# A spectral filter and a gated projection on one core: input weights requested one filter copy later, one product ahead of a transpose, second batch's units on other steps

## The chip, the cores and the metric

One core of one Trainium2 chip. The metric is device microseconds of a whole execution. The kernel before takes 787.34 us (median of 3 runs, 786.94 to 787.37).

The names used below: PE is the tensor engine (PEld its loading of weights), DVE the vector engine, ACT the scalar engine, POOL the general-purpose engine that also issues the casting DMAs, SP the engine of the sync queue. A DMA lands when the profile records its completion. The granted clock is the share of the full tensor-engine clock that the profile records as granted; 0.50 is the half clock. A turn (`a0_turn`, `z_turn`) is a transpose on PE.

## The reference

Eight sequences of 3008 tokens of 256 channels are filtered in the frequency domain, then go through a two-layer projection with a swish gate.

```python
X = np.fft.rfft(x, axis=1)                       # x: 8 x 3008 x 256
y = np.fft.irfft(X * (filt_r + 1j * filt_i), n=3008, axis=1)
h = y.reshape(24064, 256) @ w_in                 # w_in: 256 x 2048
g = h / (1 + np.exp(-beta * h))
out = g @ w_out                                  # w_out: 2048 x 256
```

## The kernel before

The transform is split by factors 47 and 64. The first batch's transform runs alone (the prologue, 0 to 37 us). Then a main part of 752 steps starts: in step s, 128 columns of `w_in` for a block of 512 tokens (`hps`), the gate on the scalar engine (`gT`), and two steps later the product with `w_out` (`acc`). Everything of the next batch's transform is placed on chosen steps of that stream. A batch is one of the eight sequences. `b` in the code counts from 0, so `b == 1` is the second batch.

The filters arrive by 24 DMAs on the sync queue, four for each of six units. Pool copies each unit's half to the other partitions (`spread`), and issues the casting DMAs (input weights `win_sb`, inputs `xg`) in the same order of program:

```python
    for u in range(3):
        spread(u)
    nc.gpsimd.dma_start(win_sb[:], moe_w_in.rearrange("(dc p) f -> p dc f", p=P))
    spread(3)
    spread(4)
    load_x(1, 0)
    spread(5)
    for g in range(1, 4):
        load_x(1, g)
    load_wout(0)          # on the sync queue, behind the filters
    load_wout(WG)
    scale_wout(0)         # on Pool: wout_sb = ws / beta
    scale_wout(WG)
    # ...
    a0_turn(4)
    a0_turn(5)
    s2_0(3)               # product with t2, then two vector products with the filters (pq_t)
    unit(2)
    # ... to s2_0(5), unit(4); then the last unit and the way to the first hps:
    s5 = [lps.tile([P, KU, P], F32, name="lp", tag="lp") for _ in range(NDC)]
    s3_0(NUN - 1, s5)     # lp: needs both vector products of unit 5
    # ... z_turn (zp), f4 (fp), then step 0 of the main part
```

The second batch's frequency units each take 2.07 us of the vector engine, and they sit on fixed steps:

```python
            s23_steps(1, [o + r for r in (21, 23, 26, 28, 30, 32, 35, 37, 39, 41, 44, 46)], 5, 1)
            # ...
            s4_steps(1, [o + 67 + (i * 12) // 15 for i in range(16)], 2)
```

## Time and profile before

| What | Before |
|---|---|
| span of the profiled run | 785.2 us |
| TensorE (PE) busy | 770.6 us |
| first hps / first acc | 36.84 / 40.76 us |
| input weights: issued / landed | 21.13 / 31.22 us |
| last filter copy on Pool starts | 30.99 us |

The head of the profile's page of the kernel before: busy time per engine, its share of the span, and instructions.

```profile
span 785.2 us, 15235 instructions
...
PE 770.6 (98%) x6046; PEld 545.0 (69%) x6046; DVE 446.7 (57%) x713; ACT 553.1 (70%) x814; POOL 150.5 (19%) x154
```

PE bounds the kernel, so what counts is where PE waits. The waits of PE, before (total us, times, longest):

```profile
PE lp L444 <- DVE pq_t L435: 3.0, 1, 3.0
...
PE acc L781 <- DVE ost L112: 0.9, 1, 0.9
...
PE ps L570 <- DVE b_t L588: 0.4, 1, 0.4
...
PE hps L763 <- ACT y L110: 0.2, 1, 0.2
```

The largest is in the prologue, and the other three shown are all that PE waits after the prologue. Busy time and gaps are not exact here, because the modelled end of a matmul can lie after the start of the next: the bar of two matmuls at 79.07 us is 0.38 us long, and the next matmul starts 0.22 us after their first. That will matter below.

The chain of waits, before, from 20 to 34 us (start, length, what), shows what the 3.0 us wait hangs on:

```profile
22.26 8.61 DMA fi_sb<-in_filt_i_dram
...
30.99 1.05 POOL fi_sb L473
...
32.06 1.30 DVE pq_t L435
...
33.40 0.41 PE lp L444 x4
```

The last filter DMA takes 8.61 us, where the DMAs of fi_sb whose landing the profile can match have a median of 4.2 us. The DMA packets tell why. They are counted here from the DMA records by start time; queue 1 is the sync queue (filters, output weights: 1 KB and 4 KB packets), queue 0 is Pool's (here 4 KB packets of the input weights).

```
before     queue 1: 1 KB / 4 KB packets   queue 0: 4 KB packets
23 to 24 us        71 / 29                        10
24 to 25 us        10 /  8                        37
25 to 26 us         0 /  0                        53
26 to 27 us        33 /  0                        44
27 to 28 us        41 /  0                        44
28 to 29 us        43 /  0                        44
```

The input weights take the DMA engines just as the last filter DMA is due. The wait has a second cost. The timeline by stretches, before (length, busy time of each engine, granted clock, DMA share, GB/s):

```profile
31.13:34.54 3.41, 0.99 (x15) 0.83 (x16) 1.77 (x3) 0.66 (x2) 2.35 (x4) 1.00 1.09 299
34.54:37.95 3.41, 3.37 (x32) 2.63 (x30) 2.63 (x9) 1.96 (x4) 2.56 (x2) 0.50 1.07 213
```

In the first stretch PE works 0.99 us of 3.41; in the next the granted clock is 0.50. The stretch at half clock is 3.41 us long. In both traces, before and after, the granted clock changes only at whole multiples of 3.413 us after its first record: before, the first record is at 7.24 us and the changes are 8 and 9 multiples later (34.54 and 37.95 us); after, it is at 5.26 us and they are 9 and 10 later (35.98 and 39.40 us). A stretch from one multiple to the next is called a window below.

### The profile page before, as it was taken

The page shows a single profiled execution, that of the slowest core. Times are in us where ns is not written, and L with a number is a line of the kernel's source. Part 1 is how long each engine was busy: PE and PEld are TensorE (multiplying, and loading weights), DVE is VectorE, ACT ScalarE, POOL GpSimd, SP SyncE. Part 2 cuts the span into 40 slices and gives each one's busy share as a digit, 9 for nine tenths or more (in the row PEclk, how much of TensorE's full clock was granted, in tenths as well). Part 3 has the DMA queues.
Part 4 walks back from the last instruction along what each step waited for, and adds up shares of the span by engine and source line. Part 5 has one row for each costly group of instructions (what it writes and reads, how often), then busy time and mean ns, then how long its engine had stood idle before and what let it go on. Part 6 is the DMA issues. An engine that isn't in the chain of part 4 may idle for free.

```text
span 785.2 us, 15235 instructions
## 1 busy us (share of the span) xinstructions
PE 770.6 (98%) x6046; PEld 545.0 (69%) x6046; DVE 446.7 (57%) x713; ACT 553.1 (70%) x814; POOL 150.5 (19%) x154
## 2 busy tenths in 40 slices
PE   8799999999999999999999999999999999999997
PEld 5566667766677666866678666786667766676665
DVE  8769754777557665566655665466655666321001
ACT  6676767767676766777667776677766777777776
POOL 6713400332012220122201222012200222000000
PEclk9999999999999999999999999999999999999999
DMA  9965586233931349123580416612164111500101
GB/s 182 241 187 122 116 229 169 68 88 99 247 85 51 96 125 252 42 76 108 114 243 28 120 61 159 197 56 86 48 189 119 63 48 48 156 28 28 55 28 55
DMA packets 84139, 88.51 MB, mean 113 GB/s; under 512 B 5772, under 2 KB 74380, under 8 KB 84068
## 3 DMA queue, kind: packets, MB, share of 16 engines
q1 hardware_dynamic: 79892, 73.81, 31.4%
q0 software_dynamic: 4032, 13.60, 10.4%
q8 instruction: 47, 0.77, 0.4%
q14 instruction: 24, 0.20, 0.1%
q10 hardware_dynamic: 144, 0.13, 0.0%
HBM read 54.47 MB, written 46.66 MB: 129 GB/s over the span
## 4 chain that ended last, share of the span: by engine, by line
PE 93%; DVE 2%; DMA 2%; SPq 0%; ACT 0%; issue 0%; POOL 0%; DVEq 0%; POOLq 0%; ACTq 0%
PE acc L781 41%; PE hps L763 41%; PE ps L554 3%; PE ps L622 2%; DMA fi_sb<-in_filt_i_dram 2%; PE ps L600 2%; PE ps L570 2%; DVE b_t L585 0%; DVE a_t L584 0%; SPq L91 0%; DVE b_t L588 0%; PE tp L400 0%; PE ps L405 0%; DVE u L224 0%; PE zp L400 0%
## 5 line engine op out<-in xcount | busy, mean ns | idle before, releaser
L772 ACT ACTIVATE gT<-hps,beta_sb 128x512 bf16<-128x512 f32 x752 | 516.9, 687 | 214.2 <-PE hps L763 211.1
L781 PE MATMUL acc<-wout_sb,gT 128*128 128x256 bf16 x3008 | 453.2, 272 | 0.9 <-DVE ost L112 0.9
L763 PE MATMUL hps<-y,win_sb 128*128 128x512 bf16 (+7 forms) x1728 | 448.6, 352 | 0.2 <-ACT y L110 0.2
L781 PEld LDWEIGHTS <-gT 128*128 128x128 bf16 x3008 | 286.8, 98 | 124.4 <-issue 2.3
L589 POOL TENSOR_TENSOR yh<-a_t,b_t 128x512 bf16<-128x512 f32 x84 | 106.3, 1266 | 426.1 <-DVE b_t L588 426.1
L763 PEld LDWEIGHTS <-win_sb 128*128 128x128 bf16 x1728 | 164.8, 98 | 24.8 <-DVE y L114 0.3
L112 DVE COPY ost<-acc 128x512 f32<-128x512 f32 (+1 forms) x94 | 60.0, 680 | 137.8 <-PE acc L781 137.8
L112 DVE CAST a<-ps 96x512 bf16<-96x512 f32 x107 | 72.8, 685 | 52.0 <-PE ps L554 47.9
L114 DVE TENSOR_SCALAR y<-ps 128x376 bf16<-128x376 f32 (+2 forms) x128 | 63.2, 511 | 62.0 <-PE ps L622 59.0
L584 DVE TENSOR_TENSOR a_t<-ps,fr_sb 128x512 f32<-128x512 f32 x84 | 58.1, 692 | 69.2 <-PE ps L570 68.6
L585 DVE SCALAR_TENSOR_TENSOR b_t<-ps,fi_sb 64x512 f32<-64x512 f32 x84 | 58.2, 693 | 1.1
L588 DVE TENSOR_TENSOR b_t<-ps,fi_sb 64x512 f32<-64x512 f32 x84 | 57.4, 684 | 1.1
L112 DVE CAST z<-ps 128x512 bf16<-128x512 f32 x72 | 49.3, 684 | 1.7 <-PE ps L600 0.8
L622 PEld LDWEIGHTS <-zz 96*128 96x128 bf16 x448 | 29.7, 97 | 22.9
L554 PE MATMUL ps<-xg,t 94*96 94x512 bf16 x112 | 42.1, 381 | 0.1
L622 PE MATMUL ps<-t,zz 96*128 96x94 bf16 x448 | 34.7, 205 | 0.0
L570 PE MATMUL ps<-a,t 128*128 128x256 bf16 x168 | 32.1, 273 | 0.4 <-DVE b_t L588 0.4
L600 PE MATMUL ps<-yh,t 128*128 128x256 bf16 x168 | 32.1, 273 | 0.0
L600 PEld LDWEIGHTS <-t 128*128 128x128 bf16 x168 | 16.2, 98 | 17.7
L570 PEld LDWEIGHTS <-t 128*128 128x128 bf16 x168 | 16.0, 98 | 15.3 <-DVE b_t L588 0.6
L171 POOL DMA_DIRECT2D xg<-in_x_dram x24 | 12.4, 519 | 56.5 <-PE ps L554 56.5
L554 PEld LDWEIGHTS <-t 94*96 94x96 bf16 x112 | 13.7, 123 | 10.2
(94 smaller groups left out, 179.0 us busy)
## 6 DMA issues: line engine op xcount, KB each, us to landing
out_dram<-ost SPq DMA_DIRECT2D x42, 512.0 KB, 3.0
d<-a SPq DMA_DIRECT2D x28, 384.0 KB, 4.5
a<-d SPq DMA_DIRECT2D x28, 384.0 KB, 5.4
d<-z SPq DMA_DIRECT2D x28, 384.0 KB, 3.9
zz<-d SPq DMA_DIRECT2D x28, 384.0 KB, 6.7
xg<-in_x_dram POOLq DMA_DIRECT2D x24, 384.0 KB, 6.4
out_dram<-ost SPq DMA_DIRECT2D x9, 256.0 KB, 3.5
ws<-in_moe_w_out_dram SPq DMA_DIRECT2D x4, 512.0 KB, 9.1
```

The source lines that it names most:

```text
L112: nc.vector.tensor_copy(dst, src)
L114: nc.vector.tensor_scalar_mul(dst, src, scale)
L554: nc.tensor.matmul(ps[:KP], lhsT=t1[:], rhs=xg[b, g][:NP, jj : jj + 2, :], start=True, stop=True)
L570: nc.tensor.matmul(ps[:, e, :], lhsT=t2[:, k0 + e, :], rhs=st["a2", b, g][:, kk + e, :], start=True, stop=True,)
L584: nc.vector.tensor_tensor(a_t[:], ps[:], fr_sb[:, ks, :], ALU.mult)
L585: nc.vector.scalar_tensor_tensor(b_t[:M], ps[M:], -1.0, fi_sb[M:, ks, :], ALU.mult, ALU.mult)
L589: nc.gpsimd.tensor_tensor(yh[:], a_t[:], b_t[:], ALU.add)
L600: nc.tensor.matmul(ps[:, e, :], lhsT=t3[:, 2 * i + e, :P], rhs=yh[:, e, :], start=True, stop=True)
L622: nc.tensor.matmul(ps[:, e, :NP], lhsT=zz[:, j0 % JG + e, dc * P : (dc + 1) * P], rhs=t4[:], start=True, stop=True,)
L763: nc.tensor.matmul(hps[:, pos - t0 : pos - t0 + ln], lhsT=win_sb[:, dc, fb * P : (fb + 1) * P], rhs=ys[b][:, dc, n0 : n0 + ln], start=(dc ...
L772: nc.scalar.activation(gT[:], hps[:], ACT.Silu, scale=beta_sb[:, fb : fb + 1])
L781: nc.tensor.matmul(acc_of(i, tb)[:, tb % 2, :], lhsT=blk[i * NFB + fb][:, tb * P : (tb + 1) * P], rhs=wout_sb[:, fb, :], start=(fb == 0 an ...
```

## The change

The intent is to let the filters finish before the input weights start, to give the vector engine unit 3's product sooner, and to take the second batch's vector work away from the steps where PE needs the vector engine for something else.

```diff
-    for u in range(3):
+    for u in range(4):
         spread(u)
     nc.gpsimd.dma_start(win_sb[:], moe_w_in.rearrange("(dc p) f -> p dc f", p=P))
-    spread(3)
     spread(4)
-    load_x(1, 0)
     spread(5)
-    for g in range(1, 4):
+    for g in range(4):
         load_x(1, g)
@@
     a0_turn(4)
-    a0_turn(5)
     s2_0(3)
     unit(2)
+    a0_turn(5)
@@
-            s23_steps(1, [o + r for r in (21, 23, 26, 28, 30, 32, 35, 37, 39, 41, 44, 46)], 5, 1)
+            s23_steps(1, [o + r for r in (22, 24, 26, 28, 30, 34, 36, 38, 40, 42, 44, 46)], 5, 1)
@@
-            s4_steps(1, [o + 67 + (i * 12) // 15 for i in range(16)], 2)
+            s4_steps(1, [o + 66 + (i * 12) // 15 for i in range(16)], 2)
```

## The prediction

> **What bounds the kernel.** PE: 770.6 of 785.2 us busy (engine table). The waits of PE in order of time: after 37 us only 0.42 us at 66.2, 0.93 at 79.1 and 0.19 at 128.5, so the rest is a fixed stream of matmuls. The prologue is a latency chain. Its largest PE wait is 2.95 us before the last filter product's turn (lp, 33.40 us), back through the vector product (pq_t, waits 2.29) and Pool's copy of fi_sb (waits 3.08) to the last filter DMA: issued 22.3, landed 30.9; the one before landed at 25.8. By DMA packets, the input weights (win, 1 MB, issued 21.13) move from 23.8 to 29.5 us: with both queues full, about 44 packets of 4 KB (win) and 43 of 1 KB (filter) start per us, one for one, so the filter gets a fifth of the bytes. [...] The wait also halves the granted clock from 34.5 to 38.0 us[...].
>
> **What the change does.** No work is added or removed.
> 1. win is issued about 23.35 instead of 21.13 us, so its packets start about 26.0, when the filters (140 KB left at 24 us, 215 KB/us) are through. Last filter landing: 30.9 to about 26.3. Pool's last copy ends 28.5 instead of 32.0.
> 2. s2_0(3) ahead of a turn: vector work starts 0.44 us earlier. Last product ends about 30.6 instead of 33.3; lp 2.75 us earlier, no half clock (about 1 us more). First hps could start near 33.3 instead of 36.84.
> 3. Batch 1's units on steps 22 to 46 leave the vector engine (2.07 us per unit) free at 33 for the accumulator copies, and its last stage ends a step before block 5 reads it: the 0.42, 0.93 and 0.19 us should go, 1.5 us together.
>
> **What is given back.** From 25 to 41 us the DMA engines are full in both versions (215 KB/us; win, x of batch 1, output weights), while PE now wants the data 3 to 4 us earlier. Estimates from the packet rates: win lands about 33.4; x group 0 about 35.4 (needed 34.8), so s1 gains only 2.9 us. Worst is the second output-weight block: before, the x requests came at 32 us and left its queue free at 32 to 34 us; now they come from 28.5, behind win without a gap, so the 1 KB packets get 42 KB/us and it lands about 42 instead of 37.2. Its scaling on Pool takes 1.9 us, so acc of fb=4, at 45.5 before and wanted near 42.5, waits until 44: a new PE wait of about 1.5 us. Net prologue gain 1.4 us.
>
> **Prediction.** 787.3 - 1.4 - 1.5 = 784.4 us; 8 in 10: 782.6 to 786.1. Faster by over 2%: 0.5%; within 2%: 99%; slower: 0.5%.
>
> **Right if** the waits for fi_sb and lp vanish, no half clock near 35 us, first hps near 33.5; a PE wait on xg or at acc behind Pool's wout scaling near 42 to 44 us; none near 66, 79, 128 us. **Wrong if** the output weights land in time (gain 4 to 5 us), or if the filters still lag behind win, the clock still halves, or later output-weight blocks stall too (little gain).

## The result and the profile after

The changed kernel takes 783.96 us (median of 4 runs, 782.81 to 785.03), before 787.31 us. The ratio is 0.9958, 95% interval 0.994 to 0.9976. Ratios here are the mean time of one kernel's runs over that of the other's of the same rounds, so not quite the ratio of the medians quoted. A second set on another chip gave 783.30 against 786.93 us, ratio 0.9956. The result is clear of noise, and inside the 2% band that counts as the same.

The four runs fall apart in two pairs: 782.81 and 783.08 us with a mean granted clock of 0.999 in both, 785.03 and 784.84 us with 0.998 and 0.996. The profiled run is one of the slower pair, so the profile shows less than the median gain.

The same lines after (source lines above are two lower after the change). The head of the page:

```profile
span 783.2 us, 15238 instructions
...
PE 769.8 (98%) x6046; PEld 543.7 (69%) x6046; DVE 446.9 (57%) x713; ACT 552.3 (71%) x814; POOL 150.6 (19%) x154
```

The waits of PE, after:

```profile
PE hps L761 <- DMA win_sb<-in_moe_w_in_dram: 1.8, 1, 1.8
...
PE lp L444 <- DVE pq_t L435: 0.2, 1, 0.2
PE ps L552 <- DMA xg<-in_x_dram: 0.2, 1, 0.2
```

The wait at lp is down from 2.95 to 0.20 us, and the three waits of the main part are gone (the list has no line for them). A new one stands at the first hps: PE now waits for the input weights. The PE timeline, after, around it (start, length, what, and idle time before it in brackets):

```profile
31.05 0.62 PE L444 MATMUL lp<-t,pq_t 128*128 128x128 bf16 x8 [0.20 <-DVE pq_t L435]
31.82 1.07 PE L400 MATMUL zp<-ident,y 128*128 128x128 bf16 x16
32.85 1.10 PE L405 MATMUL fp<-t,zz 96*128 96x94 bf16 x16
35.74 0.84 PE L761 MATMUL hps<-y,win_sb 128*128 128x512 bf16 x2 [1.79 <-DMA win_sb<-in_moe_w_in_dram]
```

lp is 2.35 us earlier than before (33.40), but the first hps only 1.10 us. In this run the window with little PE work has merely moved (stretches, after):

```profile
32.57:35.98 3.41, 1.62 (x24) 1.05 (x22) 2.16 (x8) 1.70 (x4) 1.96 (x2) 1.00 1.06 212
35.98:39.40 3.42, 3.26 (x18) 1.94 (x17) 1.37 (x2) 0.95 (x2) 0.00 (x0) 0.50 1.06 212
```

The half clock now falls on the first steps of the main part, where PE has more to do than before. The first acc starts at 40.86 us against 40.76: in the profiled run the whole prologue part is worth nothing. The gain of that run appears later. Starts of gate activations (gT, counted from 0, one for each step) in the main part, from the traces, in us:

```
                     first hps  first acc   gT 21    gT 81   last gT
before                 36.84      40.76     63.45   129.70   778.58
after                  35.74      40.86     63.56   127.73   776.61
after - before         -1.10      +0.10     +0.11    -1.97    -1.97
```

From gT 21 to gT 81 the change gains 2.08 us; after that nothing moves. So the second batch's steps are worth 2.08 us, and the prologue 0 to 2 us, depending on the run.

Why did the input weights come so late? The issue is where I expected it (23.48 us), but the transfer took longer: the DMA issues after 21 us, with KB and median us to landing, before and then after:

```profile
win_sb<-in_moe_w_in_dram POOLq DMA_DIRECT2D x1, 1024.0 KB, 10.1
ws<-in_moe_w_out_dram SPq DMA_DIRECT2D x2, 512.0 KB, 12.8
```

```profile
ws<-in_moe_w_out_dram SPq DMA_DIRECT2D x2, 512.0 KB, 7.7
win_sb<-in_moe_w_in_dram POOLq DMA_DIRECT2D x1, 1024.0 KB, 12.2
```

The output weights (`ws`) got faster and the input weights slower. By packets, after:

```
after      queue 1: 1 KB / 4 KB packets   queue 0: 4 KB packets
25 to 26 us       188 /  1                         0
26 to 27 us       254 /  0                         0
27 to 28 us       344 /  0                         0
28 to 29 us       187 /  0                        29
29 to 30 us         3 /  0                        49
30 to 31 us         5 /  0                        49
```

The first packet of the input weights starts at 28.37 us, 4.9 us after its issue; the output weights, requested at 22.92 and 23.54 us on the other queue (the second 0.06 us after the input weights), run nearly whole ahead of it, at up to 344 KB/us.

### The profile page after: what moved, and what is told of

It is laid out like the page before. It is cut to its first block, busy times and chain, and to the rows that moved or that the text cites. A ratio compares the mean times of both kernels' runs of the same rounds, so it can differ in the third digit from the quotient of the medians.

```text
span 783.2 us, 15238 instructions
## 1 busy us (share of the span) xinstructions
PE 769.8 (98%) x6046; PEld 543.7 (69%) x6046; DVE 446.9 (57%) x713; ACT 552.3 (71%) x814; POOL 150.6 (19%) x154
## 4 chain that ended last, share of the span: by engine, by line
PE 95%; DMA 2%; POOL 1%; DVE 1%; issue 1%; SPq 0%; ACT 0%; DVEq 0%; POOLq 0%
PE acc L779 42%; PE hps L761 42%; PE ps L552 3%; PE ps L620 2%; PE ps L598 2%; PE ps L568 2%; DMA xg<-in_x_dram 1%; DMA fr_sb<-in_filt_r_dram 1%; POOL fi_sb L473 1%; POOL fr_sb L472 1%; PE tp L400 0%; SPq L91 0%; PE ps L405 0%; DVE u L224 0%; DVE u L145 0%
## 5 line engine op out<-in xcount | busy, mean ns | idle before, releaser
L620 PEld LDWEIGHTS <-zz 96*128 96x128 bf16 x448 | 29.7, 97 | 22.9
```

What stands on the lines that cost most here:

```text
L620: nc.tensor.matmul(ps[:, e, :NP], lhsT=zz[:, j0 % JG + e, dc * P : (dc + 1) * P], rhs=t4[:], start=True, stop=True,)
```

## The experiments

Theory A. The two output-weight requests, in line behind the filters, hold the DMA engines until 28.3 us; the input weights follow, and PE waits for them. The wait leaves one window with little PE work (1.62 us of 3.41 in the profiled run), and the clock is halved in some runs. That it depends on where the windows happen to lie is my supposition; the traces show only that they lie differently, from 7.24 us on before and from 5.26 us on after. The steps give a fixed 2.1 us.

Rivals. B: the input weights start late because their request, made by a busy Pool, takes that long. C: the spread of the runs has nothing to do with the clock. D: the gain in the main part depends on the prologue.

### e1: the new steps alone

```diff
-            s23_steps(1, [... 21, 23, 26, 28, 30, 32, 35, 37, 39, 41, 44, 46 ...], 5, 1)
+            s23_steps(1, [... 22, 24, 26, 28, 30, 34, 36, 38, 40, 42, 44, 46 ...], 5, 1)
-            s4_steps(1, [o + 67 + ...], 2)
+            s4_steps(1, [o + 66 + ...], 2)
```

> The kernel before with only the second batch's units on their new steps; the first batch's order untouched. If the step part alone gives what the trace of the full change shows after the first accumulation (from 0.11 us behind to 1.97 us ahead), the span falls by about 2.1 us, as one narrow group of runs with a mean granted clock of 0.998 as before. If the gain depends on the new order of the first batch, less than 1 us.

Measured: 784.97 us against 787.09 (ratio 0.997, 0.9953 to 0.9986), 2.1 us by medians. In its trace gT 21 to gT 81 takes 64.16 us, before 66.25, after 64.17: 2.09 us, the same as in the full change. D falls. The runs were not narrow (783.8 to 786.69), nor were those of before on that chip (785.89 to 789.4). The profiled run, at 782.0 us of span, happened to have no half clock in the prologue: its first acc starts at 39.63 us instead of 40.76. Of those 1.1 us lp accounts for 0.2; I put the rest down to the clock. The kernel before has this chance too: on that chip its two fastest runs (785.89 and 786.11) have a granted clock of 0.999, its two slowest (789.35 and 789.4) 0.996 and 0.994.

### e2: the prologue's changes alone

The first two parts of the diff above, and not the steps.

> The kernel before with only the two changes of the first batch (input weights behind the fourth copy, fourth unit ahead of a turn). Theory[...]: the runs fall in two groups, one within 0.3 us of before with granted clock 0.998 or lower, one about 2 us faster with 0.999. Rival (the spread of the changed kernel comes from the steps or from DMA): one narrow group.

Measured: 785.44 us against 787.09 (0.9975, 0.9958 to 0.9993): 1.65 us by medians. The two groups did not appear: the runs spread from 784.41 to 786.91 us with clocks of 0.998 to 1.0. The profiled run had no half clock and still waited 1.7 us for the input weights and 1.1 us for x. So the clock is one source of spread and the landing of DMAs is another; here my expectation was too simple. The steps (2.1) and the prologue (1.65) add up to 3.8 us, where the full change measured 3.4 (medians); the intervals are wider than the difference.

### e3 and e7: idle matmuls in the new wait

```diff
         late.append((0, h, e, ps))
+    spin_late = zps.tile([P, 512], F32, name="zp", tag="zp")
+    for _ in range(6):
+        nc.tensor.matmul(spin_late[:], lhsT=rest[:, :P], rhs=rest[:], start=True, stop=True)
```

> The changed kernel with six idle matmuls (0.22 us each at full clock) between the first batch's last transform and the wait for the input weights. Theory: [...] filled, the half clock is gone in every run, all runs fall in the fast group, about 781 us of span (782.8 to 783.1 of time). Rival (the half clock comes from an earlier wait, or the two groups have another cause): still two groups, or no change.

> The changed kernel with six idle matmuls once more, so that it stands on the same chip as its neighbours: about 4.5 us faster than before, runs within 0.8 us of each other.

Measured: e3 782.85 us, runs from 782.43 to 783.18, ratio 0.9943 (0.9928 to 0.9957). e7, on another chip, 783.57 us, from 783.07 to 783.65, ratio 0.9956 (0.9943 to 0.9968). Filling the wait took the runs near 785 us away and narrowed the range from 2.2 us (changed kernel) to 0.8 and 0.6 us. e6 below has the same idle matmuls, and its five runs spread over 1.4 us (782.49 to 783.88). Taken together, three of the nine runs of the changed kernel (with e9) lie above 784.8 us, and none of the 16 of e3, e6 and e7. This supports the clock against C; the traces say more on it in the last section. A smaller gain on e7's chip than e3's is left unexplained, except that in its profiled run x landed 0.7 us later.

### e4: output weights requested after the input weights

```diff
+    held = consts.tile([1, 2], F32, name="held", tag="held")
+    nc.sync.dma_start(held[:], fi_sb[M : M + 1, 4 * KU, 0:2])   # waits for Pool's copy of unit 4
     load_wout(0)
     load_wout(WG)
```

> The changed kernel with the two output-weight requests held until Pool has copied unit 4's filters (about 26.5 us), so that they are asked for after the input weights. Theory A (the 1 MB of output weights already in the other queue keeps the engines until 28.3 us): the input weights start to move near 26 us and land near 33.5 instead of 35.7, the first matmul of the main part starts near 34, and the second output-weight block, then sharing with x, lands near 42 us, with a wait of 1 to 2 us at the accumulation of block 4. Rival B (the request itself takes 4.6 us to its first packet because Pool is busy): they still start near 28 and land near 35.7 us.

Measured: 782.87 us (0.9943, 0.9925 to 0.9961). The input weights' first packet starts at 24.87 us, 1.6 us after the issue (in the changed kernel 4.9), though Pool copies as before: B falls. They land at 32.02 us and the first hps starts at 33.84. One wait of PE in its list is much longer than in the changed kernel (there 0.2 us):

```profile
PE ps L554 <- DMA xg<-in_x_dram: 1.1, 1, 1.1
```

The wait for the input weights is gone, the wait for x is 1.1 us, and the second output-weight block lands at 41.77 us, near the prediction's 42. The wait of 1.5 us that was predicted for it at the fifth acc is only 0.21 us: that acc starts at 43.79 us (predicted 44), but PE, which has waited 1.1 us for x, comes for it at 43.58 us and not at 42.5. This kernel has the order of transfers that my prediction described, and it is no better than the one that does not: 782.87 against 782.85 us for e3 on the same chip.

### e5: idle matmuls in the old wait, old order

```diff
-    s3_0(NUN - 1, s5)
+    s3_0(NUN - 1, s5, 12)      # 12 matmuls of 512 columns between its two halves; with the new steps
```

> The kernel before with the new steps, and twelve idle matmuls in the 2.65 us wait before the second half of the last filter product's turn; the input weights are still requested early. Theory (the half clock in the first batch costs 1.1 us and is only the wait's echo): all runs are narrow, about 782.0 us of span (783.8 of time) at 0.999 or more, as the one run of the steps-only kernel without a half clock (first accumulation near 39.6 us). Then most of what the first batch's new order seems to gain is the clock, not the order. Rival (the clock has nothing to do with it): spans of 782 to 785 as in the steps-only kernel.

Measured: 784.48 us (0.9972, 0.9959 to 0.9984). Four runs lie within 0.4 us (784.13 to 784.53), one at 785.95. So four of five runs are narrow, as the clock theory says, but the fifth has the same mean clock as two of them (0.998), so the clock does not explain it; and the four are 0.4 to 0.7 us longer in span (782.4 to 782.7) than the theory said, and no better than e1 by ratio (0.9970). In its profiled run the last filter copy started at 31.31 us, later than in the profiled run of e1 (30.78), so lp was late too. Keeping the clock up does not pay for a late filter. What a half clock costs in the old order stays at the one pair of runs above.

### e6: without the move of the turn

The changed kernel with idle matmuls as in e3, and `a0_turn(5)` back ahead of `s2_0(3)`.

> The changed kernel with idle matmuls ahead of the wait for the input weights, but with the turn of unit 5 back in its old place ahead of unit 3's product. If the move of the turn matters, the last product ends about 0.4 us later and the time grows by 0.4 us against the same kernel with it. Theory (the wait for the input weights covers it): last product 0.3 to 0.4 us later, wait for the input weights that much shorter, time the same within 0.2 us.

Measured: 783.64 us, e7 on the same chip 783.57 us; ratios 0.9954 and 0.9956. The time is as expected, but not for the reason that I gave. The wait at lp is 0.57 us instead of 0.21, yet lp starts at 31.01 us instead of 30.96: the wait before unit 4's matmuls just ahead of it is shorter in exchange (1.00 us instead of 1.85). The move does bring unit 3's vector product forward, from 23.89 to 23.46 us. But the moved turn now stands ahead of unit 4's product on PE (25.46 us instead of 25.03), and unit 4's first vector product starts at 26.16 us instead of 26.23. So the move is worth 0.05 us at lp, even before the input weights land late.

### e8: output weights requested later still

As e4 with the idle matmuls of e3, but held by Pool's copy of unit 5 (`5 * KU`).

> As the last, with the output-weight requests held until Pool has copied unit 5's filters (about 28.6 us). Input weights land near 32; x group 0 near 34.5 instead of 36.2, so the wait of 1.1 us of the kernel that held them to 26.5 us goes; but the second output-weight block lands near 42.5 to 43, and the accumulation of block 4 waits 1 us or more. If DMA bytes are what binds until 42 us, the two cancel and the time is 782.5 to 783; if the order still has room, 781.5 to 782.

Measured: 790.51 us (1.0045, 1.0032 to 1.0058), 7 us slower than e7 on the same chip. My expectation failed. The first line of its list of PE waits:

```profile
PE acc L784 <- POOL wout_sb L374: 5.9, 1, 5.9
```

In e4 the first output-weight request was issued at 27.01 us, 1.5 us ahead of the first x group (28.47); here at 29.30 us, 0.7 us behind it (28.56). From 33 to 40 us the packets go one for one, about 38 to 58 of 1 KB on queue 1 and 36 to 46 of 4 KB on queue 0 in each us, and the first output-weight block lands at 42.18 us, in e4 at 33.43. The 5.9 us wait then halved the clock for 6.8 us (42.96 to 49.78 us). In e4 the output weights ran as a block as soon as the input weights were through (353 packets of 1 KB from 31 to 32 us, 1 on the other queue), ahead of x. A request 2.3 us later landed 8.7 us later. The order of the requests changed here, but it is no rule for who goes in a block: in e4 the second output-weight block was asked for at 27.46 us, ahead of x, and still shared with it.

### e9, e10, e11, e12: which order is best

e9 is the changed kernel again. e10 asks for the first 1024 columns of the input weights, then x group 0, then the other half. e11 is e10 with the output weights held as in e4, by unit 4's first copy. e12 is e10 with the second half behind x group 2.

```diff
-    nc.gpsimd.dma_start(win_sb[:], moe_w_in.rearrange("(dc p) f -> p dc f", p=P))
+    wv = moe_w_in.rearrange("(dc p) f -> p dc f", p=P)
+    nc.gpsimd.dma_start(win_sb[:, :, : FF // 2], wv[:, :, : FF // 2])
@@
     load_x(1, 0)                                                            # e12: groups 0 to 2
+    nc.gpsimd.dma_start(win_sb[:, :, FF // 2 :], wv[:, :, FF // 2 :])
```

> The changed kernel itself, beside the two that follow: about 0.995 to 0.996 of the time before, with some runs near 783 and some near 785 us. Theory (half clock by chance): the runs with a mean granted clock of 0.999 or more are the fast ones.

> The changed kernel with the input weights requested in two halves of 1024 columns, the second behind group 0 of x: the first eight steps need only the first half. If the wait for the input weights is only their landing behind 1 MB of output weights, the first half lands near 32.5 us, before it is needed at 33.9; first matmul of the main part near 33.9 instead of 35.7, x group 0 near 34.5, no wait for either, first accumulation near 37.5; the wait that let the clock be halved is gone, so the runs are narrow near 779.9 us of span (781.7 of time). If something else held it, no gain over the kernel with idle matmuls (782.9).

> As the last, with the output-weight requests held until Pool has copied unit 4's real half (about 25.4 us). The first half of the input weights starts near 25 and lands near 28.5, the output weights follow until about 31.5, x group 0 lands near 34.5. Nothing that PE needs is later than when it needs it, so the time should equal the last one within 0.3 us; if the order of backlogs is not as I think, output weights starve as in the kernel that held them to 28.6 us and the first accumulation waits 3 us or more.

> The changed kernel with the input weights in two halves, the second now behind group 2 of x instead of group 0, since group 1 was what came late (40.3 us, a wait of 1.7). Estimates from the landings seen: x groups 0 to 2 near 35, 37 and 39 us, the second half near 42 (step 8 needs it near 43), group 3 near 44.5. If the order of requests against need is the whole story, PE has no wait over 0.3 us after 34 us, the span is about 780.0 us (time 781.8) and the ratio to before about 0.993; if the bytes themselves bind, a wait turns up at the second half or at group 3 and the time stays at 782.6.

| Kernel | us, median | range | ratio to before (95%) | first hps | first acc | gT 21 |
|---|---|---|---|---|---|---|
| e9 changed | 783.30 | 783.14 to 784.97 | 0.9956 (0.9942 to 0.9969) | 34.88 | 39.14 | 61.84 |
| e10 split | 782.58 | 781.80 to 783.65 | 0.9939 (0.9925 to 0.9952) | 33.84 | 37.57 | 62.20 |
| e11 split, held | 782.69 | 782.53 to 783.81 | 0.9947 (0.9935 to 0.996) | 33.85 | 39.04 | 62.81 |
| e12 split, second half behind x group 2 | 782.74 | 782.01 to 783.09 | 0.9947 (0.9933 to 0.9961) | 33.84 | 37.69 | 61.31 |

e9 fits in part: its one run near 785 us (784.97) has the lowest clock, 0.997, but its fastest run (783.14) has 0.998 and one of 783.76 has 1.0, so the mean clock does not sort the runs as I expected. Its profiled run had no half clock: 2.18 us of PE work in the window that had 1.62 in the first profiled run, because the input weights landed 0.85 us sooner.

The splits give the first hps and, in e10 and e12, the first acc where I wanted them, but the time does not follow: 782.6 to 782.7 us instead of 781.7. In e11 x group 0 landed at 36.59 us, not near 34.5, and PE waited 1.5 us for it and 0.9 us for the next group. In e10 the wait has moved to x group 1:

```profile
PE ps L555 <- DMA xg<-in_x_dram: 1.7, 1, 1.7
```

In e12, which gives x its place back, it has moved to the third output-weight block:

```profile
PE acc L782 <- POOL wout_sb L374: 0.8, 1, 0.8
```

So the time is what the second reading of the e12 expectation said, though the wait is at another transfer than it named. In e12 the DMA engines move at least 190 KB in every us from 34 to 47 us, which fits that what one transfer gains another loses. e10 has the best median and ratio, 0.7 us below e9 on the same chip, but their intervals overlap, so "better than the change" is likely and not shown.

## Why the prediction was right and wrong

The time was right: 784.4 predicted, 783.96 measured. One large part was right for its reasons, and another only because two errors cancelled.

**Right.** PE as the bound, with only three waits after the prologue. The filters through before the input weights: Pool's last copy started at 27.65 us without a wait (predicted end 28.5, measured 28.7), lp at 31.05 us (2.35 us earlier, predicted 2.75). That most of the prologue's gain would be given back, with the DMA engines full until about 40 us in both kernels (DMA share 1.05 to 1.10 from 21 to 38 us before, 1.06 to 1.12 from 21 to 40 us after).

**Wrong, but small: "vector work starts 0.44 us earlier".** Unit 3's vector product does start earlier, but by unit 4 the lead is gone (26.26 us, before 26.23; e6 shows why). The last product ends at 31.00 us, not 30.6: this is the 0.40 us that lp fell short.

**Right in mechanism, too small in size: the step part.** Predicted 1.5 us, measured 2.08 (e1: 2.09). I summed the gaps of the waits, 0.42, 0.93 and 0.19. But a gap runs from the modelled end of one matmul to the start of the next, and ends overlap the following matmul in the undisturbed stream. The PE timeline, before, around the second wait:

```profile
77.76 0.38 PE L781 MATMUL acc<-wout_sb,gT 128*128 128x256 bf16 x2
79.07 0.38 PE L781 MATMUL acc<-wout_sb,gT 128*128 128x256 bf16 x2 [0.93 <-DVE ost L112]
79.29 0.59 PE L763 MATMUL hps<-y,win_sb 128*128 128x512 bf16 x2
```

The second pair, undisturbed by a wait inside it, takes 79.29 - 79.07 = 0.22 us from its start to the next start, though its bar is 0.38 long. The first pair took 79.07 - 77.76 = 1.31 us. The loss is 1.09 us, not 0.93. The same sum gives 0.57 for the first wait and 0.35 for the third, together 2.01 of the 2.08 measured.

**Wrong: "so its packets start about 26.0, when the filters ... are through".** They started at 28.37 us. I took the one-for-one turns that I had seen from 26 to 29 us before as a rule, though the same table shows no packet of queue 1 from 25 to 26 us, when the last filter DMA had been asked for 2.7 us earlier. The output weights, in line since 22.9 us, went first as a block, and the input weights landed at 35.69 us, not 33.4. PE waited 1.79 us for them, and the first hps started at 35.74 us, not near 33.5; x group 0 landed at 37.54 us, not 35.4. e4 shows that this is the cause: with the output-weight request held back, the first packet starts at 24.87 us.

**Wrong: "it lands about 42 instead of 37.2", and the "new PE wait of about 1.5 us" at acc.** The second output-weight block landed at 33.39 us, 3.8 us earlier than before, and no acc waits. The wait was wrong in size too: e4, where the block did land late, shows 0.21 us. It is the other face of the same error: those 1 KB packets were not starved, they did the starving.

**Wrong: "no half clock".** The wait only moved, so the window with little PE work moved too: half clock in the profiled run (35.98 to 39.40 us), none in e9's. With it the prologue is worth -0.1 us (gT 21 at 63.56 against 63.45), without it 1.6 us (61.84), each against a run of before that had its own half clock. Predicted 1.4, measured by e2's medians 1.65. The sum is near because a late input-weight landing stands where a late output-weight landing was predicted: e4, built as I had imagined the order, ends at the same time as e3, built as it was.

**Open.** What decides between a block and turns by the packet; why two equal kernels on two chips differ by 0.7 us (e3, e7); and how much of the 1.65 us is the clock and how much the order. e5 and e7 bear on it best: same chip, new steps and idle matmuls in both, old and new order. The order is worth 0.9 us by their medians (784.48 and 783.57), with intervals that overlap a little. Their profiled runs differ by 0.7 us at gT 21 (62.85 and 62.11), those of e1 and e3 on another chip by 0.9 (62.33 and 61.39), all four without a half clock.

## What to carry to other kernels

Where the DMA engines are full, look at every request that is in line on every queue before moving one: taking a transfer out of one neighbour's way can put it behind another's (here the input weights' first packet came 4.9 us after the issue), and the wait turns up at the next consumer. Cost a wait on an engine whose bars overlap in the profile from start to start against an undisturbed stretch, not from the gap (here 1.09 us lost, 0.93 us shown). And a wait of PE can cost again as half clock: the waits of 2.95 us before and 1.79 us after were followed by 3.41 us at 0.50 in those two profiled runs, the 2.6 us of e1 and 1.7 us of e2 by none, so look for two groups of runs before trusting one profile.

## What the traces show of queues, clock and gaps

- Queues. From 26 to 29 us before, turns are one for one (44 packets against 33 to 43 in each us). But in the changed kernel about 1,170 packets of 1 KB started on the other queue between the issue of the input weights (23.48 us) and their 16th packet (28.73 us), 1,117 of them before the first (28.37 us). When a queue runs as a block instead of taking turns, no run shows.
- Clock. By the profile's busy time, windows with 0.99 and 1.62 us of 3.41 were followed by half clock, one of e9 with 2.18 us was not, and one of e1 with 1.52 us (29.03 to 32.44 us) was not either; so busy time as the profile models it does not sort them. Counting columns does in the two traces before and after: cut into windows from the first clock record on, with the columns of moving data of the matmuls that start in each added up, the window of 1,920 columns (before, 31.13 us) and that of 2,784 (after, 32.57 us) were followed by half clock. The others at full clock that hold matmuls have 3,072 (before, 27.71 us) or more, and none of them was. That these two counts part them in other runs is not shown.
- Gaps. The gaps between bars mislead: 0.93 us shown, 1.09 us lost; three gaps of 1.54 us together, 2.08 us gained when they went.
